# Second MoE layer of a Nyström attention and MoE program: block transposition on VectorE through DRAM in place of TensorE transposes, with the inverse root moved to the output copy

## The chip, the core and the metric

The program runs on one core of a Trainium2 chip. The metric is device time in microseconds (us), as the median of repeated executions. The engines are named as in the profile: PE is TensorE's matmul side and PEld its weight loads, DVE is VectorE, ACT is ScalarE, POOL is GpSimd, and SP is the sync engine, which here only issues DMAs.

## The reference

Three stages in a row, all in float32. The change is in the last one, `_moe2_ref`, with 2304 tokens, d_model = 512 and d_ff = 1024.

```python
def reference(**kwargs):
    attn_out = _attn_ref(**attn_kwargs)          # Nystrom attention, 4 batches, 8 heads, 576 tokens
    x = attn_out.transpose(0, 2, 1, 3).reshape(B * S, H * D)
    x = _moe_ref(x=x, **moe_kwargs)              # g = h * tanh(softplus(h)); g @ w_out, d_ff = 2048
    return _moe2_ref(x=x, **moe2_kwargs)

def _moe2_ref(x, w_in, w_out, g_ln):
    h = x @ w_in
    h_max = np.max(h, axis=-1, keepdims=True)
    e = np.exp(h - h_max)
    sm = e / (np.sum(e, axis=-1, keepdims=True) + 1e-09)
    solu = h * sm
    mu = np.mean(solu, axis=-1, keepdims=True)
    var = np.mean((solu - mu) ** 2, axis=-1, keepdims=True)
    ln = (solu - mu) / np.sqrt(var + 1e-06) * g_ln
    return (ln @ w_out).astype(np.float32)
```

## The kernel before

The attention and the first MoE layer take the first two thirds of the program and are not touched. Their last step copies the output y of that layer out of PSUM (`ye`, line 688) and stores it to the DRAM tile `yd` (line 689, on ACT's queue).

The second MoE layer then goes over 18 tiles of 128 tokens. For each tile t:

- `load_y(t)` brings 128 tokens of y back from `yd` (line 815, on SP's queue; the first three tiles add a second part `yz`, line 821), and `split_y(t)` makes a high part on ACT (line 127) and a low part on DVE (line 128) in the tile `yb`. `yb` has two buffers, so the split of tile t+2 waits for the matmuls of tile t.
- `gemm3(t)`: 24 matmuls into `h`, a product of 128 tokens by 1024 columns over two PSUM banks (high*high, high*low and low*high). `h` has two buffers.
- `solu(t)`: the maximum of a row (DVE, line 943), exp with its sum (ACT, 945), the product with h and its sum (DVE, 948), the sum of squares around the mean (ACT, 951), an inverse square root by four Newton steps on 128x1 numbers (DVE, lines 952 to 963), and the normalised rows s (DVE, 964).
- `lnT(t)`: eight TensorE transposes of 128x128 of s into PSUM (`pt`, line 975); from there a high part `lh` (ACT, 978) and a low part `ll` (DVE, 979), four transposes at a time.
- `gemm4(t)`: 24 matmuls of `lh` and `ll` with the second weights (which carry g_ln) into `po`, a copy to `ob` (ACT, 991), and the store of 256 KB (SP, 992).

All matmuls are issued by one helper, so gemm3 and gemm4 both have line 623 in the profile; they are told apart by their output, h or po. The code writes the loop with a lag: in turn t it issues gemm3(t), solu(t), split_y(t+2), gemm4(t-3) and lnT(t-1). A scheduler then lists the instructions of each engine in an order of its own; on the chip every engine, and SP's queue of DMA issues with it, takes its list in that order, and an instruction that waits holds back all that stand behind it.

Of the kernel before, what the change touches and what calls it, by code (L numbers as in the profile page):

```python
# [22 lines left out]
def f(ap):  # L23
    return ap.bitcast(F32)
# [3 lines left out]
def nystrom_moe_kernel(  # L28
# [30 lines left out]
    F2 = w2_in.shape[1]  # L59
    NF2 = F2 // P  # L60
# [3 lines left out]
    NTT = NT // P  # L64
# [626 lines left out]
    with ExitStack():  # L691
# [49 lines left out]
        for g in range(NG):  # L741
            prep, e, c, t, a = attn(0, g)
# [70 lines left out]
        def load_y(t):  # L813
            y = (tr if p2 is None else p2).tile([P, KD, P], F32, tag="y", name="y", bufs=1 if p2 is None else 2)
            SP.dma_start(out=y, in_=yd[:, :, t * P:(t + 1) * P])
            yt[t] = y
            n = min(N - t * P, P)
            if n > 0:
                z = tr.tile([P, KD, P], F32, tag="yz", name="yz")[:, :, 0:n]
                SP.dma_start(out=z, in_=yp[:, :, t * P:t * P + n])  # L820
                V.tensor_tensor(out=y[:, :, 0:n], in0=y[:, :, 0:n], in1=z, op=ALU.add)

        def split_y(t):
            src = yt[t]
# [11 lines left out]
        for u, (s_, i) in enumerate(units):  # L836
            x = segs[s_][0] * CR // R, i // 4
# [86 lines left out]
        ps_h2 = [ctx.enter_context(tc.tile_pool(name="ps_h2a", bufs=1, space=PS, side="right"))]  # L924
        h2, ln, lt = {}, {}, {}

        def gemm3(t):
            yh, yl = yt.pop(t)
            h = ps_h2[t % len(ps_h2)].tile([P, 2, 512], F32, tag="h2", name="h2")
            for n in range(2):  # L930
                pairs = []
                for kk in range(KD):
                    vh, vl = (vi[n, kk // 2][:, kk % 2, x] for x in range(2))
                    pairs += [(yh[:, kk], vh), (yh[:, kk], vl), (yl[:, kk], vh)]
                mm3(h[:, n], pairs)
            h2[t] = h.rearrange("p a b -> p (a b)")

        def solu(t):
            h = h2.pop(t)
            st = p2.tile([P, 16], F32, tag="st2", name="st2")  # L940
            e = p2.tile([P, F2], F32, tag="e", name="e")
            s = p2.tile([P, F2], F32, tag="s2", name="s2")
            V.tensor_reduce(out=st[:, 0:1], in_=h, op=ALU.max, axis=AX.X)  # L943
            V.tensor_scalar(out=st[:, 1:2], in0=st[:, 0:1], scalar1=-1.0, scalar2=None, op0=ALU.mult)  # L944
            A.activation(out=e, in_=h, func=AF.Exp, bias=st[:, 1:2], accum_out=st[:, 2:3])  # L945
            V.tensor_scalar(out=st[:, 2:3], in0=st[:, 2:3], scalar1=1e-9, scalar2=None, op0=ALU.add)
            V.reciprocal(out=st[:, 2:3], in_=st[:, 2:3])
            V.scalar_tensor_tensor(out=s, in0=e, scalar=st[:, 2:3], in1=h, op0=ALU.mult, op1=ALU.mult,  # L948
                                   accum_out=st[:, 3:4])
            V.tensor_scalar(out=st[:, 4:5], in0=st[:, 3:4], scalar1=-1.0 / F2, scalar2=None, op0=ALU.mult)  # L950
            A.activation(out=e, in_=s, func=AF.Square, bias=st[:, 4:5], accum_out=st[:, 5:6])  # L951
            V.tensor_scalar(out=st[:, 6:7], in0=st[:, 5:6], scalar1=1.0 / F2, scalar2=1e-6,
                            op0=ALU.mult, op1=ALU.add)
            r = st[:, 7:8]
            V.tensor_scalar(out=r.bitcast(I32), in0=st[:, 6:7].bitcast(I32), scalar1=1, scalar2=None,
                            op0=ALU.logical_shift_right)
            V.tensor_scalar(out=r.bitcast(I32), in0=r.bitcast(I32), scalar1=-1, scalar2=0x5F3759DF,
                            op0=ALU.mult, op1=ALU.add)
            V.tensor_scalar(out=st[:, 6:7], in0=st[:, 6:7], scalar1=0.5, scalar2=None, op0=ALU.mult)
            for _ in range(4):  # L960
                V.scalar_tensor_tensor(out=st[:, 8:9], in0=r, scalar=st[:, 6:7], in1=r,
                                       op0=ALU.mult, op1=ALU.mult)
                V.scalar_tensor_tensor(out=r, in0=st[:, 8:9], scalar=-1.5, in1=r, op0=ALU.add, op1=ALU.mult)
            V.tensor_scalar(out=s, in0=s, scalar1=st[:, 4:5], scalar2=r, op0=ALU.add, op1=ALU.mult)
            ln[t] = s

        def lnT(t):
            s = ln.pop(t)
            lh = p2.tile([P, NF2, P], F32R, tag="lh", name="lh", bufs=3)
            ll = p2.tile([P, NF2, P], F32R, tag="ll", name="ll", bufs=3)  # L970
            for j in range(2):
                pt = ps_t.tile([P, 512], F32, tag=f"t{j}", name="pt")
                for i in range(4):
                    c = 4 * j + i
                    PE.transpose(pt[:, i * P:(i + 1) * P], s[:, c * P:(c + 1) * P], ident)  # L975
                o = slice(4 * j, 4 * j + 4)
                ptv = pt.rearrange("p (c n) -> p c n", c=4)
                A.activation(out=lh[:, o], in_=ptv, func=AF.Copy)
                V.tensor_tensor(out=ll[:, o], in0=ptv, in1=f(lh[:, o]), op=ALU.subtract)
            lt[t] = (lh, ll)  # L980

        def gemm4(t):
            lh, ll = lt.pop(t)
            po = ps_o.tile([P, DM], F32, tag="o", name="po")
            pairs = []
            for c in range(NF2):
                vh, vl = (vo[c // 2][:, c % 2, x] for x in range(2))
                pairs += [(lh[:, c], vh), (lh[:, c], vl), (ll[:, c], vh)]
            mm3(po, pairs)
            ob = p2.tile([P, DM], F32, tag="ob", name="ob")  # L990
            A.activation(out=ob, in_=po, func=AF.Copy)
            SP.dma_start(out=out[t * P:(t + 1) * P, :], in_=ob)

        gemm2(g2)
# [29 lines left out]

def _laid_out(name, a):
# [45 lines left out]
```

## Time and profile before

| | us |
|---|---|
| median of 3 runs | 659.76 (659.3 to 661.57) |
| the profiled execution, its own time | 659.22 |
| its span, from the first to the last instruction | 657.4 |
| PE busy in the span | 626.1 (95%) |
| DVE busy | 384.1 (58%) |
| ACT busy | 313.6 (48%) |

The busy times are those of one profiled execution; its own time lies 1.8 us above its span, which is what stands ahead of the first and behind the last instruction. TensorE was granted 0.975 of its full clock on average. The second MoE layer takes the span from about 445 us on.

### The profile page before, as it was taken

The numbers are of one execution on the slowest core, as the hardware profiler recorded it, in microseconds if no ns is written. First come the engines' busy times: TensorE is split into PE (matmuls) and PEld (weight loads), VectorE is DVE, ScalarE is ACT, GpSimd is POOL, SyncE is SP. The second block draws the span as 40 slices with busy tenths as digits, with TensorE's granted clock in tenths as the row PEclk, the third lists the DMA queues.
The fourth block names the chain that finished last, engine by engine and source line by source line (L and its number), as shares of the span: only waits on it lengthen the run. The fifth ranks groups of instructions, "written<-read, shape, count | busy, mean of one in ns | idle before, by whom it ended". The sixth has DMA issues, their size and how long they took to land.

```text
span 657.4 us, 11835 instructions
## 1 busy us (share of the span) xinstructions
PE 626.1 (95%) x4808; PEld 528.1 (80%) x4808; DVE 384.1 (58%) x976; ACT 313.6 (48%) x580; POOL 41.6 (6%) x21
## 2 busy tenths in 40 slices
PE   5687899999999999999997999999999999999997
PEld 2345777889889878898875999997888888888886
DVE  5899998931737235413536713457966656666560
ACT  2379985543537245424635634536534343343431
POOL 2420000000000000000005201310000000000000
PEclk9768999999999999999997999999999999999999
DMA  8998040310212010101046103213111111110001
GB/s 324 396 408 328 1 130 16 110 37 28 82 37 92 19 37 1 38 1 37 1 119 197 46 1 131 99 65 101 49 48 49 33 49 48 44 53 17 17 32 50
DMA packets 30584, 55.43 MB, mean 84 GB/s; under 512 B 3649, under 2 KB 19009, under 8 KB 30529
## 3 DMA queue, kind: packets, MB, share of 16 engines
q1 hardware_dynamic: 25344, 49.36, 21.4%
q10 hardware_dynamic: 5184, 5.31, 2.4%
q8 instruction: 38, 0.62, 0.4%
q14 instruction: 18, 0.14, 0.1%
HBM read 44.63 MB, written 10.03 MB: 83 GB/s over the span
## 4 chain that ended last, share of the span: by engine, by line
PE 85%; ACT 5%; DVE 4%; DMA 3%; issue 1%; POOL 1%; SPq 0%; POOLq 0%; ACTq 0%; DVEq 0%
PE h L623 28%; PE y L671 28%; PE po L623 15%; PE pa L612 3%; PE pt L975 2%; PE pa L298 2%; PE pa L442 2%; PE pa L353 1%; PE pa L429 1%; DMA r<-in_moe_w_in_dram 1%; POOL r L151 1%; DMA scr_w<-in_k_dram 1%; DMA r<-in_moe_w_out_dram 1%; DVE r L163 1%; ACT L648 1%
## 5 line engine op out<-in xcount | busy, mean ns | idle before, releaser
L671 PE MATMUL y<-gh,hl 128*128 128x288 f32 x1024 | 166.2, 301 | 2.4 <-ACT hl L222 1.4
L671 PEld LDWEIGHTS y<-gh,hl 128*128 128x128 f32 x1024 | 144.5, 190 | 14.1 <-issue 8.1
L623 PE MATMUL h<-AT,u 128*128 128x288 f32 x768 | 123.0, 305 | 3.7 <-ACT s L648 1.8
L623 PEld LDWEIGHTS h<-AT,u 128*128 128x128 f32 x768 | 107.9, 192 | 15.1 <-ACT u L615 4.7
L658 DVE TENSOR_TENSOR gl<-s,gh 128x288 fp32r<-128x288 f32 x128 | 55.1, 467 | 110.5 <-ACT gh L656 48.2
L623 PE MATMUL h<-hl,yb 128*128 128x512 f32 x432 | 103.2, 394 | 0.3 <-DVE s L948 0.3
L623 PEld LDWEIGHTS h<-hl,yb 128*128 128x128 f32 x432 | 79.7, 188 | 17.1 <-issue 1.0
L671 PE MATMUL y<-gl,hl 128*128 128x288 f32 x512 | 89.6, 298 | 0.0
L623 PE MATMUL po<-hl,lh 128*128 128x512 f32 x288 | 89.1, 390 | 0.0
L671 PEld LDWEIGHTS y<-gl,hl 128*128 128x128 f32 x512 | 75.0, 189 | 4.2 <-issue 3.0
L656 ACT ACTIVATE gh<-s 128x288 fp32r<-128x288 f32 x128 | 50.7, 436 | 55.6 <-PE y L671 55.3
L648 ACT ACTIVATE s<-h 128x576 f32<-128x576 f32 x64 | 41.6, 650 | 65.9 <-PE h L623 58.8
L623 PEld LDWEIGHTS po<-hl,lh 128*128 128x128 f32 x288 | 53.9, 188 | 11.1
L623 PE MATMUL po<-hl,ll 128*128 128x512 f32 x144 | 56.1, 390 | 0.0
L151 POOL TENSOR_SCALAR r<-r 128x1024 f32<-128x1024 f32 x10 | 31.6, 3162 | 363.4 <-DMA r<-in_moe_w_in_dram 303.2
L127 ACT ACTIVATE yb<-y 128x512 fp32r<-128x512 f32 x18 | 11.4, 632 | 51.0 <-PE h L623 49.5
L951 ACT ACTIVATE e<-s,st 128x1024 f32<-128x1024 f32 x18 | 20.7, 1151 | 29.6 <-DVE st L950 29.5
L943 DVE TENSOR_REDUCE st<-h 128x1 f32<-128x1024 f32 x18 | 22.0, 1223 | 21.1 <-PE h L623 16.3
L945 ACT ACTIVATE e<-h,st 128x1024 f32<-128x1024 f32 x18 | 20.1, 1117 | 28.7 <-DVE st L944 28.7
L612 PE MATMUL pa<-w,W 64*32 64x512 f32 x256 | 28.3, 643 | 5.2 <-DVE u L616 4.0
L623 PEld LDWEIGHTS po<-hl,ll 128*128 128x128 f32 x144 | 27.0, 188 | 5.6
L616 DVE TENSOR_TENSOR u<-pa,u 128x512 fp32r<-128x512 f32 x32 | 21.0, 686 | 13.9 <-ACT u L615 13.6
(168 smaller groups left out, 676.6 us busy)
## 6 DMA issues: line engine op xcount, KB each, us to landing
r<-in_moe_w_in_dram SPq DMA_DIRECT2D x8, 1024.0 KB, 8.7
ro<-in_moe_w_out_dram SPq DMA_DIRECT2D x8, 1024.0 KB, 17.8
yd<-ye ACTq DMA_DIRECT2D x32, 144.0 KB, 1.8
y<-yd SPq DMA_DIRECT2D x18, 256.0 KB, 3.1
out_dram<-ob SPq DMA_DIRECT2D x18, 256.0 KB, 2.0
w<-in_moe_w_in_dram SPq DMA_DIRECT2D x4, 1024.0 KB, 10.7
v<-in_v_dram SPq DMA_DIRECT2D x8, 512.0 KB, 4.1
r<-in_moe_w_out_dram SPq DMA_DIRECT2D x4, 1024.0 KB, 4.9
```

The source lines that it names most:

```text
L151: G.tensor_scalar(out=x, in0=x, scalar1=2.0 ** -112, scalar2=None, op0=ALU.mult)
L298: PE.matmul(out[r], lhsT=lhsT[r], rhs=rhs[r], start=True, stop=True)
L612: mm = PE.matmul(po[g][h * L:(h + 1) * L], lhsT=wb[b][r, g, h * L:(h + 1) * L], rhs=w[r, h], start=True, stop=True)
L616: V.tensor_tensor(out=u[:, 1, g], in0=po[g], in1=f(u[:, 0, g]), op=ALU.subtract))
L623: PE.matmul(o, lhsT=a, rhs=b_, start=i == 0, stop=i == n - 1)
L648: A.activation(out=s, in_=h, func=AF.Mish)
L656: A.activation(out=gh[:, e], in_=s[:, e], func=AF.Copy)
L658: V.tensor_tensor(out=gl[:, e], in0=s[:, e], in1=f(gh[:, e]), op=ALU.subtract)
L671: PE.matmul(yb[s_][d][:, 0:N], lhsT=w_out(s, i + e)[:, d * P:(d + 1) * P], rhs=r[:, e], start=i == i0 and e == k == 0, stop=i + 2 == i1 an ...
L943: V.tensor_reduce(out=st[:, 0:1], in_=h, op=ALU.max, axis=AX.X)
L945: A.activation(out=e, in_=h, func=AF.Exp, bias=st[:, 1:2], accum_out=st[:, 2:3])
L951: A.activation(out=e, in_=s, func=AF.Square, bias=st[:, 4:5], accum_out=st[:, 5:6])
```

## The change

The eight TensorE transposes of a tile go. In their place s is centred on ACT (an Identity activation with the negated mean), VectorE transposes it in blocks of 32x32 into `sT`, four DMAs store the four groups of 32 partitions into a DRAM tile (`lnd`, three of them in turn), and one DMA of 512 KB reads it back as `lT`, which is then the transposed tile. The splits into `lh` and `ll` read `lT` in SBUF, as one instruction of 1024 columns each, two turns later. The inverse root no longer scales s: it is made for two tiles at once (`root`, three Newton steps on 128x2 numbers) and scales the copy of `po` to `ob`. The PSUM that the transposes held goes to a third buffer for `h`, and the lag of gemm4 is four tiles.

```diff
+    lnd = [dram.tile([HG, HG, L, NF2 * L], F32, name=f"lnd{i}") for i in range(3)]
...
+            if t % 2 == 0:
+                vr[t // 2] = p2.tile([P, 4, 2], F32, tag="vr", name="vr", bufs=4)
+            var = vr[t // 2][:, 0, t % 2:t % 2 + 1]
             V.tensor_reduce(out=st[:, 0:1], in_=h, op=ALU.max, axis=AX.X)
...
-            A.activation(out=e, in_=s, func=AF.Square, bias=st[:, 4:5], accum_out=st[:, 5:6])
+            V.tensor_scalar(out=st[:, 4:5], in0=st[:, 3:4], scalar1=1.0 / F2, scalar2=None, op0=ALU.mult)
+            A.activation(out=s, in_=s, func=AF.Identity, scale=-1.0, bias=st[:, 4:5])
+            A.activation(out=e, in_=s, func=AF.Square, accum_out=var)
+            yield
+            sT = p2.tile([P, HG, NF2, L], F32, tag="sT", name="sT")
+            V.transpose(out=sT, in_=s.rearrange("p (c q j) -> p q c j", q=HG, j=L))
+            z = lnd[t % len(lnd)]
+            for a in range(HG):
+                SP.dma_start(out=z[a].rearrange("q j x -> j q x"),
+                             in_=sT[a * L:(a + 1) * L].rearrange("j q c i -> j q (c i)"))
+            lT = p2.tile([P, HG, NF2, L], F32, tag="lT", name="lT")
+            SP.dma_start(out=lT.rearrange("p a c i -> p a (c i)"), in_=z.rearrange("a q j x -> (q j) a x"))
+            lt[t] = lT
+            if t % 2:
+                root(vr[t // 2])
...
-            for _ in range(4):
-                V.scalar_tensor_tensor(out=st[:, 8:9], in0=r, scalar=st[:, 6:7], in1=r,
-                                       op0=ALU.mult, op1=ALU.mult)
-                V.scalar_tensor_tensor(out=r, in0=st[:, 8:9], scalar=-1.5, in1=r, op0=ALU.add, op1=ALU.mult)
-            V.tensor_scalar(out=s, in0=s, scalar1=st[:, 4:5], scalar2=r, op0=ALU.add, op1=ALU.mult)
-            ln[t] = s
...
+            for _ in range(3):
+                V.tensor_tensor(out=w, in0=r, in1=r, op=ALU.mult)
+                V.tensor_tensor(out=w, in0=w, in1=v, op=ALU.mult)
+                V.scalar_tensor_tensor(out=r, in0=w, scalar=-1.5, in1=r, op0=ALU.add, op1=ALU.mult)
...
-                    PE.transpose(pt[:, i * P:(i + 1) * P], s[:, c * P:(c + 1) * P], ident)
...
-                A.activation(out=lh[:, o], in_=ptv, func=AF.Copy)
-                V.tensor_tensor(out=ll[:, o], in0=ptv, in1=f(lh[:, o]), op=ALU.subtract)
+            A.activation(out=lhv, in_=src, func=AF.Copy)
+            V.tensor_tensor(out=llv, in0=src, in1=f(lhv), op=ALU.subtract)
...
-            A.activation(out=ob, in_=po, func=AF.Copy)
+            A.activation(out=ob, in_=po, func=AF.Copy, scale=vr[t // 2][:, 2, t % 2:t % 2 + 1])
...
-        ps_h2.append(ctx.enter_context(tc.tile_pool(name="ps_h2b", bufs=1, space=PS)))
-        ps_t = ctx.enter_context(tc.tile_pool(name="ps_t", bufs=1, space=PS))
+        for x in "bc":
+            ps_h2.append(ctx.enter_context(tc.tile_pool(name=f"ps_h2{x}", bufs=1, space=PS)))
...
-        L4 = 3
+        L4 = 4
```

What the scheduler makes of it, at three places. First PE, in the middle of the layer, between two products: po is gemm4, h is gemm3, pt the transposes. Before:

```order
L623 MATMUL po<-hl,lh 128x512 x2
L623 MATMUL po<-hl,ll 128x512
L975 MATMUL pt<-ident,s_5159 128x128 x8
L623 MATMUL h_5346<-hl,yb 128x512 x24
L623 MATMUL po<-hl,lh 128x512 x2
```

and now:

```order
L624 MATMUL po<-hl,lh 128x512 x2
L624 MATMUL po<-hl,ll 128x512
L624 MATMUL h_5724<-hl,yb 128x512 x24
L624 MATMUL po<-hl,lh 128x512 x2
L624 MATMUL po<-hl,ll 128x512
```

The eight transposes between gemm4 and gemm3 are gone, and nothing stands in their place.

Second DVE, at the start of the layer. The first reduce is tile 0's, the second tile 1's; `y<-y,yz` completes y of tile 2, which the split `yb` and gemm3 of tile 2 need. What an instruction waits for stands in brackets (DMAHW are DMAs). Before:

```order
L943 TENSOR_REDUCE st2_4945<-h2_4836 128x1 [waits PE_49]
L944 TENSOR_SCALAR st2_4945<-st2_4945 128x1 [waits DVE_49]
L821 TENSOR_TENSOR y_4940<-y_4940,yz_4942 128x4x32 [waits DMAHW0_49]
L946 TENSOR_SCALAR st2_4945<-st2_4945 128x1 [waits Activation_49]
L947 RECIPROCAL st2_4945<-st2_4945 128x1 [waits DVE_49]
L948 SCALAR_TENSOR_TENSOR s2_4947,st2_4945<-e_4946,st2_4945,h2_4836 128x1024 [waits DVE_49]
L128 TENSOR_TENSOR yb_4969<-y_4940,yb_4969 128x512 [waits Activation_49]
L950 TENSOR_SCALAR st2_4945<-st2_4945 128x1 [waits DVE_49]
L943 TENSOR_REDUCE st2_5005<-h2_4980 128x1 [waits PE_49]
```

and now:

```order
L949 TENSOR_REDUCE st2_4948<-h2_4839 128x1 [waits DMAHW3_49,DMAHW2_49,DMAHW6_49,DMAHW1_49,DMAHW7_49,DMAHW0_49,Activation_49]
L950 TENSOR_SCALAR st2_4948<-st2_4948 128x1 [waits DVE_49]
L949 TENSOR_REDUCE st2_5005<-h2_4980 128x1 [waits PE_49]
L822 TENSOR_TENSOR y_4943<-y_4943,yz_4945 128x4x32 [waits DMAHW2_49]
L950 TENSOR_SCALAR st2_5005<-st2_5005 128x1 [waits DVE_49]
L953 TENSOR_SCALAR st2_4948<-st2_4948 128x1 [waits Activation_49]
L954 RECIPROCAL st2_4948<-st2_4948 128x1 [waits DVE_49]
L955 SCALAR_TENSOR_TENSOR s2_4950,st2_4948<-e_4949,st2_4948,h2_4839 128x1024 [waits DVE_49]
L129 TENSOR_TENSOR yb_4955<-y_4943,yb_4955 128x512 [waits Activation_49]
```

The reduce of tile 1 has moved ahead of y of tile 2, and the first reduce waits for DMAs: the larger pool of this layer takes memory that the first layer's `ye` and its stores still hold. On SP's queue the load of y of tile 2 waits for the same DMAs, where before it waited for PE and POOL.

Third ACT, further on in the start of the layer. Before, `ob_5325` is the output copy of tile 1, `lh_5328` the high part of tile 3 (in two halves), `e_5372` the exp of tile 5:

```order
L991 ACTIVATE ob_5325<-po_5300 128x512 [waits PE_49]
L978 ACTIVATE lh_5328<-pt_5330 128x512 [waits PE_49]
L978 ACTIVATE lh_5328<-pt_5337 128x512 [waits PE_49]
L127 ACTIVATE yb_5395<-y_5344 128x512 [waits DMAHW7_49,PE_49]
L945 ACTIVATE e_5372,st2_5371<-h2_5346,st2_5371 128x1024 [waits DVE_49]
```

and now, where `lh_5149` is tile 1's, `ob_5271` and `ob_5365` are the output copies of tiles 0 and 1, `lh_5219` is tile 2's and `e_5302` is the exp of tile 5:

```order
L992 ACTIVATE lh_5149<-lT_5026 128x1024 [waits DMAHW1_49]
L1005 ACTIVATE ob_5271<-po_5246,vr_4951 128x512 [waits PE_49]
L951 ACTIVATE e_5302,st2_5301<-h2_5276,st2_5301 128x1024 [waits DVE_49,PE_49]
L1005 ACTIVATE ob_5365<-po_5340,vr_4951 128x512 [waits PE_49]
L992 ACTIVATE lh_5219<-lT_5101 128x1024 [waits DMAHW6_49]
L958 ACTIVATE s2_5303<-s2_5303,st2_5301 128x1024 [waits DVE_49]
```

Behind the output copy of tile 1, which waits for PE, stood the high part of tile 3, and now stands that of tile 2. On PE's list gemm4(2) follows gemm4(1) directly at this one place, without a gemm3 between them.

## Rows read from the trace of the kernel before

**Rows 1.** The page: busy time of PE; the chain that ended last, by engine.

```profile
PE 626.1 (95%) x4808; PEld 528.1 (80%) x4808; DVE 384.1 (58%) x976; ACT 313.6 (48%) x580; POOL 41.6 (6%) x21
...
PE 85%; ACT 5%; DVE 4%; DMA 3%; issue 1%; POOL 1%; SPq 0%; POOLq 0%; ACTq 0%; DVEq 0%
```

**Rows 2.** Busy time by stretch (us, engines' busy us, PEclk, DMA share, GB/s).

```profile
445.48:476.84 31.36, 31.00 (x146) 24.64 (x145) 27.34 (x91) 18.00 (x30) 0.00 (x0) 1.00 0.24 73
...
500.39:630.09 129.70, 129.70 (x618) 108.39 (x617) 82.13 (x252) 49.27 (x87) 0.00 (x0) 1.00 0.12 39
```

**Rows 3.** Chain that ended last, around one tile: start us, us, what.

```profile
477.00 5.44 PE po L623 x24
482.45 0.87 PE pt L975 x8
483.32 5.46 PE h L623 x24
488.78 1.36 PE po L623 x6
```

**Rows 4.** Timeline at the layer's start: start us, us, engine, instruction, [idle before].

```profile
445.48 5.78 PE L623 MATMUL h<-hl,yb 128*128 128x512 f32 x24
...
445.71 23.42 SPq L815 DMA_DIRECT2D y<-yd  x6
...
447.14 0.33 ACTq L689 DMA_DIRECT2D yd<-ye  x1
...
449.54 0.29 DVE L821 TENSOR_TENSOR y<-y,yz 128x128 f32<-128x128 f32 x1 [2.45 <-DMA y<-yd]
...
451.57 6.87 PE L623 MATMUL h<-hl,yb 128*128 128x512 f32 x28 [0.31 <-DVE s L948]
```

**Rows 5.** Groups by line, 477 to 640 us: busy us, mean ns of one.

```profile
L948 DVE SCALAR_TENSOR_TENSOR s<-e,st,h 128x1024 f32<-128x1024 f32 x14 | 17.9, 1281 | 0.5
L943 DVE TENSOR_REDUCE st<-h 128x1 f32<-128x1024 f32 x14 | 17.1, 1224 | 16.3 <-PE h L623 16.3
L951 ACT ACTIVATE e<-s,st 128x1024 f32<-128x1024 f32 x14 | 16.1, 1152 | 27.9 <-DVE st L950 27.9
L945 ACT ACTIVATE e<-h,st 128x1024 f32<-128x1024 f32 x14 | 15.6, 1117 | 26.8 <-DVE st L944 26.8
L961 DVE SCALAR_TENSOR_TENSOR st<-st 128x1 f32<-128x1 f32 x56 | 12.1, 217 | 1.5
...
L128 DVE TENSOR_TENSOR yb<-y,yb 128x512 fp32r<-128x512 f32 x12 | 8.2, 682 | 0.0
...
L991 ACT ACTIVATE ob<-po 128x512 f32<-128x512 f32 x14 | 8.1, 576 | 0.0
```

**Rows 6.** Groups by line, whole span: splits of 1024 columns, VectorE's transposes.

```profile
L231 DVE TENSOR_TENSOR hl<-cc,hl 128x1024 fp32r<-128x1024 f32 x4 | 4.9, 1221 | 1.2 <-ACT hl L222 1.2
L468 DVE STREAM_TRANSPOSE ATr<-Aw 128x576 f32<-128x576 f32 x6 | 4.6, 770 | 0.1
...
L222 ACT ACTIVATE hl<-cc 128x1024 fp32r<-128x1024 f32 x4 | 4.2, 1060 | 1.6 <-DVE cc L172 1.4 <-POOL r L151 0.2
L468 DVE STREAM_TRANSPOSE ATr<-Aw 128x288 f32<-128x288 f32 x4 | 1.9, 467 | 0.0
```

**Rows 7.** DMA issues, 445 to 640 us: KB each, median us from issue to landing.

```profile
y<-yd SPq DMA_DIRECT2D x16, 256.0 KB, 3.1
out_dram<-ob SPq DMA_DIRECT2D x15, 256.0 KB, 2.0
yd<-ye ACTq DMA_DIRECT2D x2, 144.0 KB, 3.4
```

**Rows 8.** Stretches of 1 us around an idle PE (columns as Rows 2).

```profile
346.00:347.00 1.00, 0.00 (x0) 0.00 (x0) 0.00 (x0) 1.00 (x3) 1.00 (x1) 1.00 0.94 317
...
349.00:350.00 1.00, 0.50 (x4) 0.20 (x8) 1.00 (x2) 0.00 (x0) 0.00 (x0) 0.50 0.10 41
...
355.00:356.00 1.00, 1.00 (x8) 0.99 (x6) 0.00 (x0) 1.00 (x3) 0.00 (x0) 0.77 0.91 334
```

More of the change, by code (lines that the diff above doesn't have):

```diff
@@ L936, in gemm3 @@
             h2[t] = h.rearrange("p a b -> p (a b)")
+        vr = {}
         def solu(t):
@@ L949, in solu @@
                                    accum_out=st[:, 3:4])
-            V.tensor_scalar(out=st[:, 4:5], in0=st[:, 3:4], scalar1=-1.0 / F2, scalar2=None, op0=ALU.mult)
-            A.activation(out=e, in_=s, func=AF.Square, bias=st[:, 4:5], accum_out=st[:, 5:6])
-            V.tensor_scalar(out=st[:, 6:7], in0=st[:, 5:6], scalar1=1.0 / F2, scalar2=1e-6,
-                            op0=ALU.mult, op1=ALU.add)
-            r = st[:, 7:8]
-            V.tensor_scalar(out=r.bitcast(I32), in0=st[:, 6:7].bitcast(I32), scalar1=1, scalar2=None,
-                            op0=ALU.logical_shift_right)
@@ L957, in solu @@
-            V.tensor_scalar(out=r.bitcast(I32), in0=r.bitcast(I32), scalar1=-1, scalar2=0x5F3759DF,
-                            op0=ALU.mult, op1=ALU.add)
-            V.tensor_scalar(out=st[:, 6:7], in0=st[:, 6:7], scalar1=0.5, scalar2=None, op0=ALU.mult)
-            for _ in range(4):
-                V.scalar_tensor_tensor(out=st[:, 8:9], in0=r, scalar=st[:, 6:7], in1=r,
-                                       op0=ALU.mult, op1=ALU.mult)
-                V.scalar_tensor_tensor(out=r, in0=st[:, 8:9], scalar=-1.5, in1=r, op0=ALU.add, op1=ALU.mult)
@@ L964, in solu @@
-            V.tensor_scalar(out=s, in0=s, scalar1=st[:, 4:5], scalar2=r, op0=ALU.add, op1=ALU.mult)
-            ln[t] = s
-        def lnT(t):
-            s = ln.pop(t)
+            V.tensor_scalar(out=st[:, 4:5], in0=st[:, 3:4], scalar1=1.0 / F2, scalar2=None, op0=ALU.mult)
+            A.activation(out=s, in_=s, func=AF.Identity, scale=-1.0, bias=st[:, 4:5])
+            A.activation(out=e, in_=s, func=AF.Square, accum_out=var)
+            yield
+            sT = p2.tile([P, HG, NF2, L], F32, tag="sT", name="sT")
@@ new lines, in solu, with root @@
+            if t % 2:
+                root(vr[t // 2])
+        def root(x):
+            v, r, w = x[:, 1], x[:, 2], x[:, 3]
+            V.tensor_scalar(out=v, in0=x[:, 0], scalar1=0.5 / F2, scalar2=0.5e-6, op0=ALU.mult, op1=ALU.add)
+            V.tensor_scalar(out=r.bitcast(I32), in0=v.bitcast(I32), scalar1=1, scalar2=None,
+                            op0=ALU.logical_shift_right)
+            V.tensor_scalar(out=r.bitcast(I32), in0=r.bitcast(I32), scalar1=-1, scalar2=0x5EF759DF,
+                            op0=ALU.mult, op1=ALU.add)
+            for _ in range(3):
+                V.tensor_tensor(out=w, in0=r, in1=r, op=ALU.mult)
+                V.tensor_tensor(out=w, in0=w, in1=v, op=ALU.mult)
+                V.scalar_tensor_tensor(out=r, in0=w, scalar=-1.5, in1=r, op0=ALU.add, op1=ALU.mult)
@@ L969, in lnT, with split_ln @@
+        def split_ln(t):
+            src = lt[t].rearrange("p a c i -> p c a i")
             lh = p2.tile([P, NF2, P], F32R, tag="lh", name="lh", bufs=3)
             ll = p2.tile([P, NF2, P], F32R, tag="ll", name="ll", bufs=3)
[L971 to L974, printed above, removed]
-                    PE.transpose(pt[:, i * P:(i + 1) * P], s[:, c * P:(c + 1) * P], ident)
-                o = slice(4 * j, 4 * j + 4)
-                ptv = pt.rearrange("p (c n) -> p c n", c=4)
-                A.activation(out=lh[:, o], in_=ptv, func=AF.Copy)
-                V.tensor_tensor(out=ll[:, o], in0=ptv, in1=f(lh[:, o]), op=ALU.subtract)
+            lhv, llv = (x.rearrange("p c (a i) -> p c a i", a=HG) for x in (lh, ll))
+            A.activation(out=lhv, in_=src, func=AF.Copy)
+            V.tensor_tensor(out=llv, in0=src, in1=f(lhv), op=ALU.subtract)
@@ L1012, in nystrom_moe_kernel @@
                     gemm3(t)
-                solu(t)
+                x = solu(t)
+                next(x)
             if t + 2 < NTT:
                 split_y(t + 2)
+            if t < NTT:
+                next(x)
+            if 2 <= t <= NTT + 1:
+                split_ln(t - 2)
+            if t < NTT:
+                spin(x)
             for _ in range(3 if t < L4 else 100):
@@ L1020, in nystrom_moe_kernel @@
                 gemm4(t - L4)
-            if 1 <= t <= NTT:
-                lnT(t - 1)
 def _laid_out(name, a):
```

## The prediction

> **What bounds the kernel now.** The page first: PE is busy for 95% of the span and is 85% of the chain that ended last [rows 1]. So I looked for the layer that changes in busy time by stretch. In its steady part, 500.39 to 630.09 us, PE is busy for all of 129.70 us, while DVE fills 82.13 and ACT 49.27 [rows 2]: whatever leaves PE there is time saved, as long as the others keep up. The chain of waits around one tile shows PE's own period: 24 matmuls of gemm4 in 5.44 us, the transposes, 24 of gemm3 in 5.46, and the next gemm4 at 488.78, 11.78 after the one at 477.00 [rows 3]. A matmul is thus 5.46 / 24 = 0.2275 us, and what the eight transposes take from PE is 11.78 - 5.44 - 5.46 = 0.88 us a tile. The start is another matter: from 445.48 to 476.84 DVE is busy for 27.34 of 31.36 us [rows 2], so there a reordered DVE can hold PE back.
>
> **The transposes go.** 18 tiles x 0.88 = 15.8 us off PE.
>
> **The other engines in the steady part.** DVE's transpose of 1024 columns does not occur before. Its rows are 0.770 us for 576 and 0.467 for 288 columns [rows 6]; a straight line through them gives 1.24 for 1024, the 576 row itself is the bound below, 0.467 x 1024 / 288 = 1.66 the bound above, and I take 1.24. The low part becomes one instruction from SBUF, 1.22 by line 231 [rows 6]. Per tile DVE then has the reduce 1.22, the product 1.28, the transpose 1.24, ll 1.22, the low part of y 0.68 [rows 5, 6], some five small ones and half a root (12 instructions for two tiles), at 0.2 each with their gaps (line 961 takes 0.217 [rows 5]): about 2.2. Together 7.8 of a new period of 10.9. ACT: exp 1.12, Identity (priced as the square) 1.15, square 1.15, lh 1.06 by line 222, yb about as ob, ob 0.58 [rows 5, 6], with two accumulator reads: 6.1. SP has seven issues in place of two, and 1.0 MB a tile more to move. A store of 256 KB lands in 2.0 us, a load of 256 KB in 3.1 [rows 7]; for four stores of 128 KB I take 2.0 (bound above 3.4, the slowest store shown; below, nothing lands in less than 2.0 there), for the load of 512 KB 3.6 (3.1 to 6.2, twice the row). From h(t) to the end of its transpose I count 7.1 us on DVE and ACT; lT(t) stands on SP behind the first store of tile t+1, a period of 10.9 later, which covers t's own stores; issues take 0.9, the load 3.6, lh and ll 2.3. That is about 25 us, and gemm4(t) comes four periods, 43 us, after h(t). So all of it lies under PE's work. The third h buffer and the lag cost nothing for the same reason. In the tail the last chain, some 19 us, lies under four gemm4s of 5.46. Cost: nothing.
>
> **The start of the layer.** Here I walked the lists of the changed kernel with the durations above. Times are the old span's, all estimates.
>
> First wait. Before, PE got through gemm3(1) at 445.48 + 5.78 = 451.26 and then lost 0.31 us, to the product of tile 0; y of tile 2 was complete at 449.83 [rows 4]. Now the load of that y and the first reduce wait for the last `ye` store to land. It was issued at 447.14 [rows 4] and could go 0.2 earlier; landing takes 2.0 to 3.4 [rows 7], and I take 449.3. The load issued then lands at 452.9 (3.1 [rows 7] to 3.8, as in 445.71 to 449.54 [rows 4]). On DVE the reduce of tile 1 stands ahead and runs from 451.4 to 452.6, then y is complete at 453.2. Its high part on ACT lets PE start at 453.95, for two matmuls. PE's next row is a matmul of gemm3(3), whose high part stands on ACT behind the exp of tile 1: 455.75. The low part of tile 2 stands on DVE behind the product of tile 0: 455.7. PE runs on from 456.0, having done three matmuls in 4.7 us: lost 4.05.
>
> Then 76 matmuls, to 473.3. Meanwhile DVE, by the ends of its larger instructions: low y(3) 456.55, product(1) 458.25, transpose(0) 459.5, transpose(1) 462.2 (Identity(1) on ACT ends at 460.9), reduce(2) 463.4, low y(4) 464.2, the root of tiles 0 and 1 with small ones 466.9, product(2) 468.2, reduce(3) 469.45, low y(5) 470.3, transpose(2) 472.15 (Identity(2) at 470.85), product(3) 473.85, reduce(4) 475.05, ll(0) 476.65. ACT has exp(3) to 472.15, square(2) to 473.45 and only then lh(0), to 474.55. PE waits for lh(0) for 1.3 and, after six more matmuls, for ll(0) for 0.75; gemm4(1) starts at 484.65.
>
> By then: transpose(3) 477.95; the root of tiles 2 and 3 has to wait for square(3) at 479.0, behind exp(4); product(4) 481.35, rest of the root 483.3. ACT: Identity(4) 482.9, square(4) 484.2, lh(1) 485.3; ll(1) 486.6. PE loses 0.65 and 0.85 and ends gemm4(1) at 491.65. gemm4(2) follows at once; its lh stands on ACT behind exp(5), done by 490.55, and behind the copy of gemm4(1)'s output, 492.3, so lh(2) is there at 493.4: 1.8 lost, and 0.75 more until ll(2) at 494.65. From gemm3(6) on the walk finds no further wait: lh is then two tiles ahead.
>
> Sum of waits: 4.05 + 1.3 + 0.75 + 0.65 + 0.85 + 1.8 + 0.75 = 10.15. The old start had some too: 31.36 [rows 2] for 120 matmuls (27.3) and three sets of transposes (2.64), so 1.4. The start costs 10.15 - 1.4 = 8.7 us more. Bounds: the first wait alone, 4.05 - 1.4 = 2.6, if the later parts come a little earlier; and with the transpose at 1.66, five of them in the chain, 8.7 + 2.1 = 10.8.
>
> **The sum** on the profiled execution: 659.2 - 15.8 + 8.7 = 652.1. It lies 0.5 under the median of the runs shown, so I give **652.5**.
>
> **A rule weighed.** The trace says eight transposes cost PE 0.88 us [rows 3], and VectorE's way is a chain of some 8.9 us (transpose 1.24, issues 2.1, stores 2.0, load 3.6, the estimates above). The Trainium skill ("VectorE: DVE Perf Modes", Rules for kernel authors) sends a 128x128 transpose to TensorE where the result may lie in PSUM, and notes (The three transpose paths) that VectorE transposes only within 32x32 blocks. By it the change loses 8.0 us a tile, which is rival 4 in full. In this trace PE has no free time in the steady part and DVE has 36% [rows 2], so the sum goes by the rows.
>
> **Rivals.**
> 1. Only the first wait remains. For it: the later waits are 0.65 to 1.8 us each, and each hangs on estimates of that size. Against it: gemm4(2)'s lh stands behind gemm4(1)'s copy whatever the durations. 659.2 - 15.8 + 2.6 = 646.0.
> 2. TensorE's clock falls in the first wait. PE stood still from before 346 until 349.5; it then ran at 0.50, the level of 1.2 GHz, and was back at full only after 355 [rows 8]. Seven us at half speed lose 3.5. Against it: here three matmuls come in between and no idle piece is over 2.7 us. 652.5 + 3.5 = 656. The Trainium skill ("TensorE: Matmul & The Clock Gate", HAM oscillation) says that gaps between groups of matmuls bring the clock down again; the rows agree.
> 3. Slower: the clock stays at half through the start, because waits come again every 10 us. A matmul of 0.2275 us then takes twice that; the gain of 7 us is gone after 7 / 0.2275 = 31 matmuls at half clock, and with 60 the time is 652.5 + 13.7 = 666. For it: the one long wait shown held the clock down for 7 us. Against it: between the waits PE runs for 17 and 8 us without a pause.
> 4. Slower: the way through DRAM comes late in every tile. PE begins to wait once lT is some 18 us later than I have it, five times the load's 3.6; with the whole chain of 8.9 us open in each of 18 tiles it would be 659.2 - 15.8 + 160 = 803. Against it: 256 KB land in 3.1 us and the DMA engines are busy for 0.12 of the steady part [rows 2, 7]. The rule weighed above is this case.
> 5. Start and saving cancel: the later waits come out twice as long (6.1 us more) beside a slow first one: 659.
>
> **Chances.** Forecast (650 to 655) 0.52; rival 1 (644 to 650) 0.25; rival 2 (655 to 657.7) 0.11; rival 5 0.06; rival 3 0.05; rival 4 0.01. A change of under 0.3%, 2 us, can't be told from none by three runs. Faster is the forecast with rivals 1 and 2, 0.88; same 0.06; slower 0.06. The range leaves out rivals 3 to 5 and the low end of rival 1: 645.0 to 657.5.
>
> **What would show it.** Steady period 10.9 us, PE without gaps from about 505 on, no pt line. At the start PE idle from 451.3 for over 2 us, ended by ACT yb, then waits on lh and ll of tiles 0 to 2, some 10 us in all. If the steady period is longer than 10.9, DVE, ACT or the DRAM way is the bound and I am wrong there; if the waits sum to under 5, I over-walked the start. A granted clock under 1 between 451 and 500 is rival 2 or 3.

## The result and the profile after

The changed kernel took 654.46 us (median of 4 runs, 653.28 to 654.84), the kernel before, run with it, 659.53 (658.61 to 661.57). The ratio is 0.9916, 95% interval 0.9889 to 0.9943: 0.8% faster. The profiled execution of after took 653.28 us, with a span of 651.3; it was the fastest of the four, 1.2 us under their median.

The page of after, with the rows that answer to [rows 1], two groups and two kinds of DMA that are new:

```profile
PE 613.6 (94%) x4664; PEld 515.8 (79%) x4664; DVE 375.9 (58%) x850; ACT 332.8 (51%) x580; POOL 40.5 (6%) x21
...
PE 83%; ACT 6%; DVE 5%; DMA 3%; issue 2%; POOL 1%; SPq 0%; ACTq 0%; POOLq 0%; DVEq 0%
...
L993 DVE TENSOR_TENSOR ll<-lT,lh 128x1024 fp32r<-128x1024 f32 x18 | 22.0, 1222 | 15.0 <-ACT lh L992 14.9
L962 DVE STREAM_TRANSPOSE sT<-s 128x1024 f32<-128x1024 f32 x18 | 22.4, 1244 | 14.0 <-ACT s L958 14.0
...
lnd<-sT SPq DMA_DIRECT2D x72, 128.0 KB, 2.8
lT<-lnd SPq DMA_DIRECT2D x18, 512.0 KB, 4.2
```

PE has 144 matmuls fewer (4664 against 4808), the transposes, and is 12.5 us less busy. The steady part, as chain and as stretch (columns as in [rows 3] and [rows 2]); the first of the two stretches is the start of the layer:

```profile
555.11 5.44 PE po L624 x24
560.54 5.44 PE h L624 x24
565.99 5.44 PE po L624 x24
```

```profile
446.56:502.13 55.57, 50.34 (x206) 39.60 (x204) 37.46 (x94) 30.49 (x44) 0.00 (x0) 0.94 0.55 154
544.06:620.00 75.94, 75.94 (x337) 62.90 (x336) 49.45 (x107) 39.50 (x56) 0.00 (x0) 1.00 0.53 156
```

gemm4 to gemm4 is 10.88 us where it was 11.78 [rows 3], without a gap; DVE is at 65% there and ACT at 52%. The start is the other half of the story: 55.57 us for the 203 matmuls that start in it (206 touch it), which take 46.2 at 0.2275 each, so 9.4 us lost. The timeline of after at that place, which answers to [rows 4]:

```profile
449.79 1.28 ACT L951 ACT_TABLE_LOAD   x1 [1.85 <-DMA yd<-ye]
449.88 1.23 DVE L949 TENSOR_REDUCE st<-h 128x1 f32<-128x1024 f32 x1 [8.20 <-DMA yd<-ye]
449.95 7.39 SPq L816 DMA_DIRECT2D y<-yd  x4
...
452.38 1.23 DVE L949 TENSOR_REDUCE st<-h 128x1 f32<-128x1024 f32 x1 [1.09 <-PE h L624]
453.52 0.28 DVE L822 TENSOR_TENSOR y<-y,yz 128x128 f32<-128x128 f32 x1
...
453.83 0.63 ACT L128 ACTIVATE yb<-y 128x512 fp32r<-128x512 f32 x1 [1.31 <-DVE y L822]
...
454.56 0.81 PE L624 MATMUL h<-hl,yb 128*128 128x512 f32 x2 [2.22 <-issue]
...
456.13 6.11 PE L624 MATMUL h<-hl,yb 128*128 128x512 f32 x14 [0.76 <-DVE st L957]
```

The first reduce and the loads of y (SPq) start only when the last `ye` store (yd<-ye) has landed; y of tile 2 is complete at 453.80, its high part is made next, and PE stands still for 2.22 us, does two matmuls, and stands still again for 0.76, until the high part of tile 3 is there (ACT ends it at 456.08; the row names a small DVE instruction that ended then too). The first reduce starts 3.3 us into the layer (449.88 - 446.56). Before it started 0.2 us in, and so it does in e2 (no transposes) and e4 (the new root) below; with two h buffers (e6) or a lag of three (e7) it still starts 3.4 us in. What is left of the change to bring this wait are the new tiles of the pool, sT and lT. What PE's clock did, in stretches of 2 us (PEclk is the number behind POOL's):

```profile
452.00:454.00 2.00, 0.34 (x2) 0.00 (x0) 1.59 (x5) 0.69 (x3) 0.00 (x0) 1.00 0.73 216
454.00:456.00 2.00, 0.81 (x2) 0.30 (x2) 1.97 (x5) 2.00 (x4) 0.00 (x0) 0.75 0.00 0
456.00:458.00 2.00, 1.87 (x4) 1.49 (x5) 1.93 (x6) 1.90 (x3) 0.00 (x0) 0.50 0.12 30
458.00:460.00 2.00, 2.00 (x6) 1.61 (x5) 1.57 (x4) 0.87 (x3) 0.00 (x0) 0.50 0.78 232
460.00:462.00 2.00, 2.00 (x6) 1.52 (x6) 1.21 (x1) 1.91 (x3) 0.00 (x0) 0.54 0.74 162
462.00:464.00 2.00, 2.00 (x11) 1.61 (x10) 0.04 (x1) 0.00 (x0) 0.00 (x0) 1.00 0.89 207
```

It fell to 0.50, the level of 1.2 GHz, in the wait and stayed there until shortly before 462: six matmuls touch a stretch of 2 us where eleven do at full clock. The 77 matmuls from 456.13 to 476.40 took 20.27 us and would take 17.5, so 2.8 us went there. Further on PE waits once more, for the high and the low part of tile 2:

```profile
491.57 0.69 ACT L1005 ACTIVATE ob<-po,vr 128x512 f32<-128x512 f32 x1 [1.77 <-PE po L624]
492.16 1.05 ACT L992 ACTIVATE lh<-lT 128x1024 fp32r<-128x1024 f32 x1
...
493.26 0.73 PE L624 MATMUL po<-hl,lh 128*128 128x512 f32 x2 [1.72 <-ACT lh L992]
...
494.52 0.50 PE L624 MATMUL po<-hl,ll 128*128 128x512 f32 x1 [0.52 <-DVE ll L993]
```

The output copy of tile 1 waits for PE, and the high part of tile 2 stands behind it on ACT. These are the only two waits of PE behind 470 us.

From the first matmul of gemm3(1) to the end of the last one, the layer took 208.1 us before (445.48 to 653.60) and 201.0 after (446.56 to 647.59): 7.1 less. The unchanged part ahead of it ended 1.1 us later in this execution; in the profiled executions below, which all share that code, it ended anywhere between 444.35 and 447.05. Layer times compare better than spans, and all below are taken like this one.

### The profile page after: what moved, and what is told of

Read it like the earlier page. It is cut to its first block, busy times and chain, and to the rows that moved or that the text cites. A ratio compares the mean times of both kernels' runs of the same rounds, so it can differ in the third digit from the quotient of the medians.

```text
span 651.3 us, 11585 instructions
## 1 busy us (share of the span) xinstructions
PE 613.6 (94%) x4664; PEld 515.8 (79%) x4664; DVE 375.9 (58%) x850; ACT 332.8 (51%) x580; POOL 40.5 (6%) x21
## 4 chain that ended last, share of the span: by engine, by line
PE 83%; ACT 6%; DVE 5%; DMA 3%; issue 2%; POOL 1%; SPq 0%; ACTq 0%; POOLq 0%; DVEq 0%
PE h L624 30%; PE y L672 29%; PE po L624 14%; PE pa L613 4%; PE pa L299 2%; PE pa L443 1%; PE pa L430 1%; DMA r<-in_moe_w_in_dram 1%; POOL r L152 1%; PE pa L354 1%; DMA scr_w<-in_k_dram 1%; DMA r<-in_moe_w_out_dram 1%; ACT r L155 1%; DVE lmk L342 1%; ACT L649 1%
## 5 line engine op out<-in xcount | busy, mean ns | idle before, releaser
L624 PEld LDWEIGHTS h<-AT,u 128*128 128x128 f32 x768 | 109.4, 194 | 14.7 <-ACT u L616 4.7
L624 PE MATMUL h<-hl,yb 128*128 128x512 f32 x432 | 105.3, 399 | 3.1 <-issue 2.2
L624 PEld LDWEIGHTS h<-hl,yb 128*128 128x128 f32 x432 | 82.5, 192 | 22.7 <-issue 2.6
L958 ACT ACTIVATE s<-s,st 128x1024 f32<-128x1024 f32 x18 | 20.7, 1152 | 21.3 <-DVE st L957 21.2
L993 DVE TENSOR_TENSOR ll<-lT,lh 128x1024 fp32r<-128x1024 f32 x18 | 22.0, 1222 | 15.0 <-ACT lh L992 14.9
L962 DVE STREAM_TRANSPOSE sT<-s 128x1024 f32<-128x1024 f32 x18 | 22.4, 1244 | 14.0 <-ACT s L958 14.0
```

The source lines that it names most:

```text
L958: A.activation(out=s, in_=s, func=AF.Identity, scale=-1.0, bias=st[:, 4:5])
L962: V.transpose(out=sT, in_=s.rearrange("p (c q j) -> p q c j", q=HG, j=L))
L993: V.tensor_tensor(out=llv, in0=src, in1=f(lhv), op=ALU.subtract)
```

## The experiments

In their expectations theory T is the account above. U says that DVE and ACT bound the start whatever the first wait does, V that the way through DRAM, the lag or the root matters more than the transposes on PE. The kernel before, run beside each group of kernels, took 660.21, 659.83 and 660.02 us.

**e1: y of tile 2 ahead of the layer.** On the changed kernel:

```diff
-            y = (tr if p2 is None else p2).tile([P, KD, P], F32, tag="y", name="y", bufs=1 if p2 is None else 2)
+            if p2 is None:
+                y = tr.tile([P, KD, P], F32, tag="y2nd" if t == 2 else "y", name="y", bufs=1)
...
         split_y(1)
+        load_y(2)
+        split_y(2)
...
-            if t + 2 < NTT:
+            if t and t + 2 < NTT:
                 load_y(t + 2)
```

> The changed kernel, with y of tile 2 loaded and split ahead of the layer, from the pool that no `ye` store holds (yb gets a third buffer). Nothing is left out. Theory T (the changed kernel loses 3.46 us to its first wait, because the load of y of tile 2 and the first reduce wait for the last `ye` store, and 2.8 us more to the clock that falls in that wait): gemm3(2) follows gemm3(1) without the pieces of 2.2 and 0.8 us, the granted clock stays at its upper level, and the time is 654.5 - 3.5 - 2.8 = 648.2 us (646.5 to 650). Theory U (DVE and ACT bound the start anyway, so that the wait only moves to the high and low parts of tiles 0 and 1, 3.55 us by the prediction's walk): 654.5 - 6.3 + 3.6 = 651.8 us (651 to 655).

Measured: 645.43 us (643.93 to 646.51), ratio to before 0.9771 (0.9741 to 0.9801), 1.1 under T's range. The layer took 194.5 us, 6.5 less than in the changed kernel; T said 6.3. Of the 9 us between the medians another 1.2 lie ahead of the layer, and 1.2 are what the profiled execution of the changed kernel lies under its median. gemm3(2) followed gemm3(1) without a gap at full clock, and the view of waits on PE in the layer has one row left:

```profile
PE po L624 <- DVE ll L996: 1.5, 2, 0.9
```

These two pieces are for the low parts of tiles 2 and 3. U is out: with the first wait gone, no wait for the parts of tiles 0 and 1 came up. It was close at tile 0, whose low part was ready at 475.17 and was taken at 475.23.

**e5: the wait filled.** On the changed kernel, 16 matmuls behind gemm3(1) whose result nobody reads:

```diff
+                    if t == 1:
+                        po = ps_o.tile([P, DM], F32, tag="o", name="po")
+                        vh = vi[1, 0][:, 0, 0]
+                        mm3(po, [(yh[:, kk % KD], vh) for kk in range(16)])
```

> The changed kernel, with 16 more matmuls that nobody reads, into an output buffer that is free then, directly behind gemm3(1): they fill the first wait and change nothing else. Nothing of the output is left out. Theory T (the clock fell because PE stood still; that cost 2.8 us beside the wait of 3.46): PE is busy through the wait, the granted clock stays at its upper level, and 2.8 us come back: 654.5 - 2.8 = 651.7 us (650.5 to 653). Theory U (PE is then ahead of DVE and ACT again, and meets the waits for the high and low parts of tiles 0 and 1 that the prediction walked, 3.55 us): 654.5 us or more, with these waits on PE.

Measured: 651.96 us (650.42 to 652.56), 2.5 under the changed kernel, T's number. PE's timeline has no gap up to 489, and the stretch where the clock had been at 0.50 is at 1.00. The 79 matmuls behind the filler start at 456.18, where the changed kernel had 77 of them left at 456.13:

```profile
446.82 5.77 PE L624 MATMUL h<-hl,yb 128*128 128x512 f32 x24
452.43 3.91 PE L624 MATMUL po<-hl,yb 128*128 128x512 f32 x16
456.18 18.07 PE L624 MATMUL h<-hl,yb 128*128 128x512 f32 x79
```

```profile
456.00:458.00 2.00, 2.00 (x11) 1.64 (x10) 1.93 (x6) 1.89 (x3) 0.00 (x0) 1.00 0.06 12
458.00:460.00 2.00, 2.00 (x10) 1.69 (x9) 1.84 (x4) 0.86 (x3) 0.00 (x0) 1.00 0.84 249
```

So the clock fell because PE stood still, and that fall was worth some 2.5 us beside the wait itself. The low part of tile 0 was ready at 475.27, 0.2 us ahead of the matmul that reads it (475.45): U is wrong here too, though by little. Up to the second wait, the one for the high part of tile 2, the layer was 2.6 us ahead of the changed kernel's (44.14 us from its start to the matmul behind the wait, against 46.70). In this profiled execution that wait brought the clock down as well (see the last section), which took 1.6 back: the whole layer is 200.0 us, 1.0 under the changed kernel's.

**e9: the same edit on the kernel before.**

> The kernel before with the edit of e1 alone (y of tile 2 loaded and split ahead of the layer). Output as it was. It asks whether e1's 9 us are a gain of their own, or only undo a wait that the change made. Theory T (the kernel before waits for 0.31 us there and its first reduce for no `ye` store, so there is nothing to win): 659.8 us within 1.2. Rival (starting the layer earlier is worth as much there as in the changed kernel): 655 us or less.

Measured: 659.97 us (10 runs), ratio 0.9997 (0.9983 to 1.0011). As T said: the 0.31 us wait of before is gone, and nothing else moves (the layer took 207.9). e1's 9 us are no gain of their own: they undo what the change does to the start.

**e2: the transposes left out of the kernel before**, so that its output is that of another matrix.

```diff
+            sv = s.rearrange("p (c n) -> p c n", c=NF2)
...
-                    PE.transpose(pt[:, i * P:(i + 1) * P], s[:, c * P:(c + 1) * P], ident)
...
-                A.activation(out=lh[:, o], in_=ptv, func=AF.Copy)
+                A.activation(out=lh[:, o], in_=sv[:, o], func=AF.Copy)
```

> The kernel before, with the second layer's transposition left out: the high and low parts are made from the product s itself, so that the output is that of another matrix. This prices what the eight transposes a tile take, with root, lag and pools as they were. Theory T (they take 0.88 us of PE a tile, 18 times): 659.5 - 15.8 = 643.7 us (642.5 to 645), with a period of about 10.9 us in the steady part. Theory V (the transposes lie in time in which PE would wait anyway, and what the change gained came from the root or the lag): over 650 us.

Measured: 647.16 us (645.94 to 647.86), 3.5 above T. The layer took 195.5 us, 12.6 less than before. The period in the steady part is 10.88, as T said; what is missing stands at the end, where gemm4(16) waits for an output buffer whose copy stands on ACT behind the last tile's sum of squares:

```profile
629.43 0.98 PE L623 MATMUL po<-hl,lh 128*128 128x512 f32 x2 [1.86 <-ACT ob L987]
```

The granted clock then was 0.50 and 0.71 in the next two stretches of 2 us, which costs 1.6. 12.6 + 1.9 + 1.6 = 16.1: the transposes are worth what they take on PE, 15.8 to 16. A lag of three tiles, good enough with transposes in PE's list, leaves the end open without them.

**e7: a lag of three on e1.**

> Kernel e1 (645.4 us) with a lag of three tiles in place of four. Theory T (the way through DRAM takes 25 us, and three periods are still 32.6): no wait in the steady part; at the end the last tile's low part is ready 19.3 us after its h (620.4 to 639.7 in the changed kernel), and three gemm4s cover 16.4, so that PE waits for some 2.9 us in two pieces and its clock may fall: 645.4 + 2.9 = 648.3, up to 650 with the clock (647 to 651). Rival V (the way is near its limit at a lag of four): waits in each tile, over 660 us.

Measured: 648.67 us (647.03 to 650.68), 3.2 above e1, as T said. The steady part has no wait; at the end there are the two that T named, and the clock went to 0.59 and 0.56:

```profile
636.93 0.73 PE L624 MATMUL po<-hl,lh 128*128 128x512 f32 x2 [1.77 <-ACT lh L995]
638.19 0.67 PE L624 MATMUL po<-hl,ll 128*128 128x512 f32 x1 [0.53 <-DVE ll L996]
```

**e10: a lag of five on e1**, with a fourth buffer for the parts.

> Kernel e1 (645.4 us) with a lag of five tiles and a fourth buffer for the high and low parts. What is left to win in e1 is the wait for the low parts at the start, 1.5 us in two pieces. Theory T (with one more tile of lag, gemm4 comes a tile after its high and low parts are made, and the end is covered as it was): the steady period stays 10.88, the two waits go, 643.9 us (642.5 to 645). Rival (lag buys nothing beyond four, since PE is full from 500 us on and gemm4(2) still follows gemm4(1) without a gemm3 between): 645.4 us, or 1 to 2 slower through waits that only move.

Measured: 645.32 us (643.08 to 646.20), the same as e1. The two waits for low parts went, and one of 1.11 us for an output copy came at 507.8. T was wrong and the rival right: a fifth tile buys nothing.

**e6: two h buffers on e1.**

```diff
-        for x in "bc":
+        for x in "b":
```

> Kernel e1 (y of tile 2 early, 645.4 us) with two buffers for h in place of three. Theory T (the third buffer matters at the start alone, where gemm3(2) would wait for the product of tile 0): that product ended at 454.16 in e1 and gemm3(1) at 450.9, so PE waits for 3.2 us, and its clock falls again, up to 2.8 us more: 651.4 us (648.5 to 653), with a steady period of 10.88 as before. Rival (the buffer is worth nothing): 645.4 us within 1. Rival (it is needed in every tile): over 655 us.

Measured: 647.64 us (646.92 to 648.22), 2.2 above e1. The wait is the one that T computed, at the product of tile 0 (it ended at 453.58):

```profile
453.74 1.48 PE L624 MATMUL h<-hl,yb 128*128 128x512 f32 x4 [3.18 <-DVE st L956]
```

The clock fell (0.60 and 0.54 in two stretches of 2 us, 1.7 lost). But T's sum was 3.8 too high: with two buffers a whole gemm3 stands between gemm4(1) and gemm4(2) in PE's list, and e1's two waits for low parts (1.5) are gone with that; the clock cost 1.1 less than T put; some 1.2 stays open. So the third buffer is worth 2 us, at the start alone.

**e4: the root alone.** The kernel before with s centred on ACT, the root for two tiles and the scaled output copy; transposes, lag and buffers as before.

> The kernel before with one part of the change alone: the product is centred on ACT, the inverse root is made for two tiles at once with three iterations and scales the output copy. The transposes stay on PE, the lag stays three tiles, there are two h buffers. Theory T (this part takes work from DVE where PE, not DVE, is the bound): 659.5 us, within 1 (658.5 to 660.5). Theory V (this part gives the gain): 655 us or less.

Measured: 659.52 us (10 runs), ratio 0.999 (0.9974 to 1.0005), the layer 208.2. DVE is busy for 30 us less in the layer and ACT for 18 more; PE, which bounds it, does the same. Before, and e4:

```profile
445.48:653.60 208.12, 207.76 (x986) 172.00 (x984) 132.79 (x413) 82.42 (x144) 0.00 (x0) 1.00 0.14 45
```

```profile
445.62:653.79 208.17, 207.60 (x986) 172.19 (x984) 102.58 (x287) 100.31 (x162) 0.00 (x0) 1.00 0.14 44
```

That part of V is out.

**e3: twice through DRAM.** On the changed kernel:

```diff
+            z2 = lne[t % len(lne)]
+            SP.dma_start(out=z2, in_=lT.rearrange("p a c i -> p (a c i)"))
+            lT = p2.tile([P, HG, NF2, L], F32, tag="lT2", name="lT2")
+            SP.dma_start(out=lT.rearrange("p a c i -> p (a c i)"), in_=z2)
             lt[t] = lT
```

> The changed kernel, with each transposed tile stored to DRAM and loaded back a second time before it is split: a store and a load of 512 KB more per tile, on the same queue. Output as it was. Theory T (the way through DRAM takes 25 of the 43 us that the lag gives, and some 8 us more still fit): steady period still 10.88 us, 654.5 us, with the start perhaps 2 later (653.5 to 657). Theory V (the way through DRAM or its traffic bounds something): the way gets 8 us longer in each tile or holds SP's queue, so that PE waits in the steady part: over 660 us.

Measured: 706.74 us (704.82 to 708.83), 52 above the changed kernel. T was far out, and V's "over 660" came true. PE waited nine times for a high part, and its clock kept falling (the mean was 0.947 in this execution, 0.967 in the changed kernel's):

```profile
PE po L625 <- ACT lh L997: 25.8, 9, 5.6
PE po L625 <- DVE ll L998: 6.0, 9, 0.7
```

But see what one such high part, that of tile 9, waited for. Its second load was issued and took 4.3 to 4.6 us to land, by 584; it was split 16 us later, when ACT came to it in its list, behind the output copy and the Identity of tile 12:

```profile
579.14 0.34 SPq L973 DMA_DIRECT2D lT<-lne  x1
```

```profile
597.86 0.69 ACT L1010 ACTIVATE ob<-po,vr 128x512 f32<-128x512 f32 x1 [1.59 <-PE po L625]
...
598.44 1.14 ACT L959 ACTIVATE s<-s,st 128x1024 f32<-128x1024 f32 x1
599.48 1.04 ACT L997 ACTIVATE lh<-lT 128x1024 fp32r<-128x1024 f32 x1
...
600.58 0.73 PE L625 MATMUL po<-hl,lh 128*128 128x512 f32 x2 [2.76 <-ACT lh L997]
```

The longer way moved the high part back in ACT's list, and there it closes a circle: PE waits for it, and it waits for work that follows from PE's last h. The queue of SP is in order too: it stood for 33.7 us for first loads to land (11 times) before it could issue the second stores, with the next tile's stores behind:

```profile
SPq L971 <- DMA lT<-lnd: 33.7, 11, 4.1
```

Which of the two did more, this run does not separate. That DRAM itself is no bound in the steady part, e8 shows.

**e8: the second trip on POOL's queue**, on e1.

```diff
+            G.dma_start(out=z2, in_=lT.rearrange("p a c i -> p (a c i)"))
...
+            G.dma_start(out=l2.rearrange("p a c i -> p (a c i)"), in_=z2)
```

> Kernel e1 (645.4 us) with the second trip through DRAM of e3, but its store and load issued on POOL's queue, where nothing else stands. The split reads what comes back the second time. Theory T (e3 lost its 52 us because the trip's two waits stood in SP's queue, ahead of the stores and loads of the next tiles, and the high part in ACT's list behind the Identity of a later tile, not because DRAM or the DMA engines were full): the way gets some 8 us longer, lies under four periods, and the steady period stays 10.88: 645.4 us, up to 5 more at the start (644 to 651). Theory V (the traffic of 1 MB more a tile, or 8 us more of latency, is what DRAM can't hide): over 660 us.

Measured: 666.32 us (663.68 to 670.44), 21 above e1, above T's 651 and on V's side of 660. Three stretches (in the start, in the steady part, at the end):

```profile
476.00:501.79 25.79, 20.74 (x80) 15.39 (x79) 13.99 (x31) 11.98 (x18) 3.22 (x6) 0.93 0.97 302
501.79:600.00 98.21, 98.21 (x435) 81.33 (x434) 57.21 (x130) 46.01 (x65) 9.14 (x17) 1.00 0.72 222
...
625.00:662.20 37.20, 27.22 (x90) 20.05 (x88) 8.73 (x23) 8.87 (x12) 2.68 (x5) 0.82 0.52 162
```

In the steady part T holds to the digit: PE is busy for all of 98.21 us, with twice the trips and 222 GB/s, so neither the traffic nor the longer way is a bound there. The 21 us lie at both ends; at the end, four gemm4s are all the cover there is. From the last reduce to the end of the last low part it is 31.4 us (623.84 to 655.27), against 19.3 in the changed kernel; the trip added 12, not 8. From the reduce to the landing of the last load it is 25.3 us where it was 16.0, since the stores and loads beside it took longer too (first loads 5.0 where they were 4.2). That load landed at 649.1, and some 3 us more went by on ACT, where the last high part stands behind the output copy of tile 16 and so waits for PE, which then has only that part's product left:

```profile
652.38 0.69 ACT L1013 ACTIVATE ob<-po,vr 128x512 f32<-128x512 f32 x1 [7.72 <-issue]
652.97 1.04 ACT L1000 ACTIVATE lh<-lT 128x1024 fp32r<-128x1024 f32 x1
```

PE idles for 10 us at the end and 5 at the start, and runs at a lower clock after each. V is out for the tiles in the middle, and T had left out the ends.

## Why the prediction was right, and where it was not

The median lies 2.0 above the predicted 652.5, inside the range. In the profiled execution the layer became 7.1 us shorter, which is the sum's own difference (15.8 - 8.7); the 2.0 are the 1.1 us ahead of the layer and the 1.2 that this execution lies under its median, less the 0.4 that the prediction had added for its own. The saving was right by its mechanism; the cost at the start came out right in part by luck. Behind that:

- **The transposes go**: right, in size too. 11.78 became 10.88, and e2 prices the transposes alone at 16 us, where 15.8 were summed. Each tile got 0.90 us shorter. The Trainium skill ("VectorE: DVE Perf Modes", Rules for kernel authors) would leave the transposes on TensorE; for this kernel, where TensorE is the bound and VectorE is not, the measurement decides against it.
- **The other engines**: the new transpose took 1.244 us (1.24 by the line through two shorter ones), ll 1.222, Identity 1.152. DVE had 7.1 us a period (49.45 over 75.94 / 10.88 periods) where 7.8 was summed, ACT 5.7 where 6.1 was.
- **The way through DRAM**: right, hidden in every tile. Its stores took 2.8 (2.0 taken, bound 3.4), its load 4.2 (3.6 taken, bound 6.2), and loads of y rose from 3.1 to 4.2 beside them. The last tile's chain took 19.3 us, "some 19" there, under 21.8 of gemm4s. That is a margin of 2.5 us, and e7 and e8 show what lies beyond it.
- **The first wait**: right in place and cause, and nearly in size. 3.3 us (456.13 - 452.34 - two matmuls) against 4.05; the two pieces had two matmuls between them, not three.
- **The step that failed**: the waits for lh(0), ll(0), lh(1) and ll(1), 3.55 us in all. None came, but for 0.1 at ll(1). The walk of DVE's list was too slow: it had ll(0) ready 31.2 us after the layer's start (476.65 - 445.48), and in e5, where PE was not late, it was ready after 28.5 (475.27 - 446.82). The 2.7 us grew step by step, 1 by the end of product(1), 2 by the end of the root. Four waits of 0.65 to 1.3 us hung on it. (In the changed kernel itself ll(0) was ready after 31.0 us, since the slow matmuls held the reduce of tile 2 back by 2.32 us; PE was late as well, and found it ready.)
- **What took their place**: rival 2, the clock. It fell in the first wait in spite of the matmuls in between, and cost 2.5 to 2.8 us (e5, and the 77 matmuls) where 3.5 was put. It had 0.11. So the total at the start came out as predicted, 9.4 against 10.15, out of other parts, and that is luck: PE stood idle for 5.2 us of it (2.22 + 0.76 + 1.72 + 0.52) where the prediction had some 10, and the clock made up most of the rest.
- **lh(2) and ll(2)**: right. 1.72 + 0.52 us against 1.8 + 0.75, behind the copy ob(1) on ACT; and with a gemm3 between the two gemm4s (e6) they are gone.
- **The third buffer and the lag cost nothing**: true, and they buy something: 2 us (e6) and 3 us (e7), at the ends.

The change with its first wait taken away (e1) is, with e10, the best of the kernels here, 2.3% under before. Its layer has PE busy for 192.96 of 194.53 us.

## What to carry to other kernels

When work left the engine that is the bound, the steady part gained just what that engine's rows said, and the rest was decided at the start and the end of the loop, where there is no cover: look there for the first thing that the new buffers, waits and list order make late. A larger pool can be a wait: here it took memory from stores still on their way, and moving one small load and its split ahead of it took another 6.5 us off the layer, where the change itself had taken 7.1. The walk through an engine's list, with each small instruction rounded up, drifted by a tenth (2.7 us of 28.5); take waits that come out of it smaller than that drift as undecided.

## What the runs showed of the hardware

**The clock and short idle pieces.** PE's granted clock fell to 0.50 after idle pieces of 2.22 + 0.76 us (after), 3.18 (e6), 1.86 (e2) and 1.77 + 0.53 (e7), and was back at full 3 to 7 us later. But the same wait, 1.72 + 0.52 us for the high and low part of tile 2, left it alone in the changed kernel and brought it down in e5. The first row is after, the second e5, each just behind that wait:

```profile
494.00:496.00 2.00, 1.48 (x6) 1.24 (x7) 1.85 (x5) 1.97 (x5) 0.00 (x0) 1.00 0.62 201
```

```profile
494.00:496.00 2.00, 2.00 (x6) 1.54 (x6) 1.72 (x10) 0.60 (x1) 0.00 (x0) 0.50 0.75 114
```

The same two pieces left it alone in e8 too, as did one of 1.53 us there. What a short wait costs through the clock could not be told ahead of the run here. The Trainium skill ("TensorE: Matmul & The Clock Gate", HAM oscillation) describes a kernel in which the wait between groups of matmuls brings the clock down each time; here some waits did so and others of the same size did not.

**A scaled output copy costs more.** The copy of po to ob took 0.576 us before [rows 5] and 0.679 with a scale from a column of SBUF, for the same 128x512; in e4, with transposes and buffers as before, the median is 0.670.
